# Retention attention and a maxout network: one plain feature block instead of two in the second tile, the weight sums moved forward, and the sums put in another order

## The chip, the cores and the metric

The kernel runs on one core of a Trainium2 chip. The metric is the device time of one execution in microseconds; a kernel's time is the median of its runs. In the profile PE is TensorE (PEld its weight loads), DVE is VectorE, ACT is ScalarE, POOL is GpSimd and SP is the queue that issues most of the transfers.

## The reference, cut to what matters

```python
# attention: batch 8, heads 8, seq 576, head_dim 64
scores = scale * np.matmul(q, k.transpose(0, 1, 3, 2))
Dmat = np.where(rel >= 0, gamma[:, None, None] ** rel[None, :, :], 0.0)
x = np.matmul(scores * Dmat, v)                 # then (B,H,S,D) -> (B*S, H*D)
# network: 4608 tokens, d_model 512, d_ff 768
h = np.maximum(np.maximum(x @ w1, x @ w2), x @ w3)
out = h @ w_out
```

The weights come in as 64-bit floats and are turned into 32-bit floats on the chip. All arithmetic that concerns us is in 32-bit floats.

## The kernel before, in words

**Tiles and blocks.** The 4608 tokens are cut into nine tiles `t` of 512. The 768 hidden features are cut into six blocks `fb` of 128. For each tile the function `ffn(t)` computes the hidden values `h[:, fb, :]` block after block, and then multiplies them by `w_out` (`downs`). Attention for the next tile (`scores`, `state`, `values`, `transposes`) is threaded in between: `ffn` is a generator that yields at set points, and the main loop (L755) issues the attention steps of `steps(t + 1)` at these points. Nothing is reordered later: each engine runs its instructions in the order in which the program issued them.

**Plain and fast blocks.** A block needs a product of a 2x4 grid (two halves of the tile's tokens by four chunks of d_model; the pieces are called `a11` to `a24`) with a 4x3 grid (four chunks by three weight matrices; `b11` to `b43`). Done plainly this is 24 small products. `up_plain` does it so: one triple (i = 0, 1, 2) of four 512-column products each. `up` does it with 20 products of 256 columns (`PRODUCTS`) at the price of sums before and after them. The sums of x (`X_SUMS`, 13 VectorE instructions for each tile, L335) and the sums of w (`W_SUMS`, 19 instructions, done in place in the weights, L530) come before. After the products, ScalarE copies partial results out of PSUM (L564), and VectorE joins them in 14 instructions (`JOINS`, L559), two of which write the block's hidden values: `lo` for the first 256 tokens (at product B6) and `hi` for the others (at product A7). The first tile (t = 0) is all plain, since its weights are still being converted. The second tile (t = 1) has two plain blocks, 2 and 3. From then on all blocks are fast.

**Accumulators.** A plain triple takes PSUM tiles from the pool `ps_x` (even fb) or `ps_y` (odd fb), each with two buffers. A fast block takes its chains A and B from `ps_x` and E, C and D from `ps_y`. A buffer comes free when its last reader is done: for a plain product with i = 0 a ScalarE copy (L604), for i = 1 and 2 a VectorE maximum (L603).

**Chores.** Sums that can wait are put into a queue `chores`, and `chore(n)` issues n of them. `urgent` is a second queue that goes first. Both mostly feed VectorE, and what is issued stands in VectorE's line before whatever comes after it.

**The down product.** `downs` computes `h @ w_out` by seven products over 2x2 grids, each over the three pairs `fp` of blocks. Product 1 (`dx`, L424) takes for each pair the `lo` half of the even block (e = 0) as its weights; product 2 (`dy`) takes the `lo` half of the odd block (e = 1). Products 3, 5, 6 and 7 take sums of the hidden values (`sums_of_hidden`, L400 to L402).

**Order of the blocks.** Two, three, zero, one, four, five in the second tile, and zero, one, four, five, two, three in all later tiles (L635).

Of the kernel before, what the change touches and what calls it, by code (L numbers as in the profile page):

```python
# [53 lines left out]
FILL = 224  # L54
PARTS = 20

X_SUMS = """s19 = a12 + a14, s15 = s19 - a22, s3 = a22 - a12, s10 = s3 - a13, s13 = a12 + a13, s20 = s10 + a23,
            s14 = a24 - s15, s11 = s20 + a24, s11 = a21 - s11, s7 = s11 - s13, s6 = s19 + s7,
            s16 = a11 - s11, s16 = s16 - a14"""
W_SUMS = """b33 = b13 + b33, n1 = b13 + b43, n2 = n1 - b41, n3 = b11 - n2, n4 = b33 - b32, b43 = b43 + n4,  # L60
            b23 = b43 - b23, b43 = b41 - b43, n5 = b22 + b23, b41 = b41 - n5, b21 = b21 - b41,
            b23 = b32 + b23, b22 = b22 - b21, b32 = b22 - b32, n6 = b31 + n2, n7 = b42 + n4,
            b42 = b42 - n5, b31 = b31 + b32, n8 = b12 - n4"""

PRODUCTS = """E a11 b12, E a14 b42, B s15 n5, A a22 b21, C s3 b23, B s19 b41, A s10 b32, C a13 b31, B s6 n2, A s13 b22,
              C a11 b11, B s14 n1, A s11 n4, D s7 b43, B a23 n6, A s20 b33, D s16 b13, B a21 n3, A a21 n8, A a24 n7"""
# [6 lines left out]
         "A7": [("A1", ("A1", "B6"), ALU.add), ("A1", ("A1", "A5"), ALU.max), ("hi", ("A1", "A7"), ALU.max)]}  # L73
X_SUMS, W_SUMS = ([x.split() for x in text.split(",")] for text in (X_SUMS, W_SUMS))
PRODUCTS = [x.split() for x in PRODUCTS.split(",")]
# [4 lines left out]
def kernel(  # L80
# [91 lines left out]
    late, chores, urgent, spread = {}, deque(), deque(), []  # L172

    def chore(n=1):
        for _ in range(n):
            if urgent or chores:
                (urgent or chores).popleft()()  # L177

    def soon(step):

        if spread:
            urgent.append(step)
        else:
            step()  # L184
# [135 lines left out]
    def output(chunks, o, t, i):  # L320
# [9 lines left out]
        if i == CPT - 1 and t > 0:  # L330
# [4 lines left out]
            def step(n, dst, _, a, sign, b):  # L335
                combine(*(xS[t][x] for x in (dst, a, b)), sign)
                if dst not in (later[0] for later in X_SUMS[n + 1:]):
                    made[t].add(dst)

            for n, line in enumerate(X_SUMS):  # L340
                soon(partial(step, n, *line))

    def combine(dst, a, b, sign):
        nc.vector.tensor_tensor(dst, a, b, op=ALU.add if sign == "+" else ALU.subtract)
# [31 lines left out]
    def sums_of_outs():  # L376

        pool = late["pool"]
        lo, hi = slice(0, DM // 2), slice(DM // 2, DM)
        b11, b12, b21, b22 = (w_out[:, :, e, r] for e in range(2) for r in (lo, hi))  # L380
        t1, t2, t4 = (pool.tile([P, NF // 2, DM // 2], FP32, name=f"To{n}")[:] for n in (1, 2, 4))

        def on_vector(fp):
            nc.vector.tensor_tensor(t1[:, fp], b12[:, fp], b11[:, fp], op=ALU.subtract)
            nc.vector.tensor_tensor(t2[:, fp], b22[:, fp], t1[:, fp], op=ALU.subtract)

        def on_gpsimd(fp):
            nc.gpsimd.tensor_tensor(b12[:, fp], b22[:, fp], b12[:, fp], op=ALU.subtract)
            nc.gpsimd.tensor_tensor(t4[:, fp], b21[:, fp], t2[:, fp], op=ALU.subtract)

        for fp in range(NF // 2):
            chores.extend([partial(on_vector, fp), partial(on_gpsimd, fp)])
        late["T"] = {1: b11, 2: b21, 3: b22, 4: t4, 5: t1, 6: t2, 7: b12}
        late["S"] = {n: pool.tile([P, NF // 2, NH], FP32, name=f"H{n}") for n in (1, 2, 3, 4)}
# [126 lines left out]
    def factor(name, fb):  # L521

        if name[0] == "n":
            return late["W"][int(name[1]) - 1][:, fb, :]
        d, i = int(name[1]) - 1, int(name[2]) - 1
        return w_up[i][:, fb, d * P:(d + 1) * P]

    summed_fp = set()

    def weight_sums(fp):  # L530

        def step(dst, a, sign, b):
            combine(*(factor(n, slice(2 * fp, 2 * fp + 2)) for n in (dst, a, b)), sign)

        for dst, _, a, sign, b in W_SUMS:
            chores.append(partial(step, dst, a, sign, b))
        chores.append(partial(summed_fp.add, fp))

    def late_room():
        pool = late["pool"]  # L540
        late["W"] = [pool.tile([P, NF, P], FP32, name=f"n{n}") for n in range(1, 9)]
        late["X"] = {n: pool.tile([P, NH], FP32, name=n)[:] for n in sorted({x[0] for x in X_SUMS})}

    converting = convert_all()

    def convert(n):
        for _ in range(n):
            next(converting, None)
# [35 lines left out]
    def downs_plain(t, h):  # L584

        ps = [(ps_x, ps_y)[m % 2].tile([P, DM], FP32, tag="xy"[m % 2], name="down") for m in range(NT // P)]
        for fb in range(NF):
            for m, b in enumerate(ps):
                nc.tensor.matmul(b[:], lhsT=h[:, fb, m * P:(m + 1) * P], rhs=w_sb["out", fb],
                                 start=(fb == 0), stop=(fb == NF - 1))  # L590
                if fb == NF - 1:
                    osb = opool.tile([P, DM], FP32, tag="osb", name="osb")
                    nc.scalar.copy(osb[:], b[:])
                    nc.sync.dma_start(out[t * NT + m * P:t * NT + (m + 1) * P, :], osb[:])
            yield

    def up_plain(t, h, fb, i):
        ps = (ps_x, ps_y)[fb % 2].tile([P, NT], FP32, tag="xy"[fb % 2], name="up")
        for dc in range(NDC):
            nc.tensor.matmul(ps[:], lhsT=w_sb[i, fb][:, dc * P:(dc + 1) * P], rhs=xT[t][:, dc, :],  # L600
                             start=(dc == 0), stop=(dc == NDC - 1))
        if i > 0:
            return lambda: nc.vector.tensor_tensor(h[:, fb, :], h[:, fb, :], ps[:], op=ALU.max)  # L603
        return lambda: nc.scalar.copy(h[:, fb, :], ps[:])  # L604

    def ffn(t):

        h = hpool.tile([P, NF, NT], FP32, tag="h", name="h")
        if t == 0:
            for fp, i in units:  # L610
                for fb in (2 * fp, 2 * fp + 1):
                    maximum = up_plain(t, h, fb, i)
                    convert(4)
                    maximum()
                yield
            convert(6)
            for fb, _ in enumerate(downs_plain(t, h)):
                convert(4 if fb < 2 else 4 * len(pieces))
                if fb == 2:
                    while_converting.close()  # L620
                    late["pool"] = ctx.enter_context(tc.tile_pool(name="late", bufs=1))
                    late_room()
                    sums_of_outs()
                elif fb > 2:
                    chore(2)
                if fb in (1, 3):
                    yield
            yield
            return
        if t == 1:  # L630
            spread.append(True)
            weight_sums(0)
            weight_sums(2)
        plain = (2, 3) if t == 1 else ()
        order = (2, 3, 0, 1, 4, 5) if t == 1 else (0, 1, 4, 5, 2, 3)  # L635
        total = sum(24 if fb in plain else len(PRODUCTS) for fb in order)
        count = parts = 0
        for n, fb in enumerate(order):
            if fb not in plain:
                while fb // 2 not in summed_fp:  # L640
                    chore()
            steps_of_one = up_plain_all(t, h, fb) if fb in plain else up(t, h, fb)
            for step, cost in enumerate(steps_of_one):
                if fb in plain:
                    chore(8)
                elif step % 2 or step % 5 == 4:
                    chore(len(urgent) > 0)
                elif step % 4 == 2 and chores:
                    chores.popleft()()
                count += cost or 1  # L650
                if count * (NF // 2 * 3) >= (parts + 1) * total:
                    parts += 1
                    yield
            if n % 2:
                sums_of_hidden(h, fb // 2)
                if fb in plain:
                    weight_sums(fb // 2)
        chore(len(urgent))
        for n, _ in enumerate(downs(t, h)):
            chore(4)  # L660
            if n in (1, 3):
                yield
        yield

    def up_plain_all(t, h, fb):
        for i in range(3):
            up_plain(t, h, fb, i)()
            yield 8
# [86 lines left out]
    for t in range(N // NT):  # L755
        work = ffn(t)
        for todo in steps(t + 1):
            for step in todo:
                step()
            next(work, None)  # L760
# [51 lines left out]
```

## Time and profile before

| | |
|---|---|
| median of 3 runs | 781.73 us (780.21 to 782.14) |
| span of the profiled run | 777.6 us |
| PE busy | 767.2 us, 99% |
| DVE busy | 569.7 us, 73% |
| ACT busy | 326.0 us, 42% |
| POOL busy | 101.9 us, 13% |
| granted TensorE clock | 1.00 |
| second tile, plain blocks | 124.50 to 147.28 us on PE |
| second tile, fast blocks | 147.28 to 189.90 us on PE |

The first tile ends at about 124 us of the span; each later one takes about 82 us. The busy time of PE is modelled for the ends of its instructions, so its gaps are read from the starts of instructions that follow each other.

### The profile page before, as it was taken

The page shows a single profiled execution, that of the slowest core. Times are in us where ns is not written, and L with a number is a line of the kernel's source. Part 1 is how long each engine was busy: PE and PEld are TensorE (multiplying, and loading weights), DVE is VectorE, ACT ScalarE, POOL GpSimd, SP SyncE. Part 2 cuts the span into 40 slices and gives each one's busy share as a digit, 9 for nine tenths or more (in the row PEclk, how much of TensorE's full clock was granted, in tenths as well). Part 3 has the DMA queues.
Part 4 walks back from the last instruction along what each step waited for, and adds up shares of the span by engine and source line. Part 5 has one row for each costly group of instructions (what it writes and reads, how often), then busy time and mean ns, then how long its engine had stood idle before and what let it go on. Part 6 is the DMA issues. An engine that isn't in the chain of part 4 may idle for free.

```text
span 777.6 us, 14439 instructions
## 1 busy us (share of the span) xinstructions
PE 767.2 (99%) x5000; PEld 624.4 (80%) x5000; DVE 569.7 (73%) x1248; ACT 326.0 (42%) x808; POOL 101.9 (13%) x124
## 2 busy tenths in 40 slices
PE   8899999999999999999999999999999999999998
PEld 7545444588888888888888888888888888888887
DVE  2998989889667857785769657876778567855672
ACT  3664641154155514452345234532544054524651
POOL 3110112101101201111111111110112001200000
PEclk9999999999999999999999999999999999999999
DMA  9995544333233332343233333333333323001001
GB/s 224 231 236 130 155 109 104 59 58 59 73 69 59 58 67 62 62 78 68 60 56 59 57 94 59 58 58 96 59 56 59 72 54 72 11 14 42 2 1 54
DMA packets 236939, 59.33 MB, mean 76 GB/s; under 512 B 217921, under 2 KB 235585, under 8 KB 236865
## 3 DMA queue, kind: packets, MB, share of 16 engines
q1 hardware_dynamic: 236432, 58.14, 34.9%
q8 instruction: 39, 0.64, 0.3%
q10 hardware_dynamic: 432, 0.27, 0.1%
q14 instruction: 36, 0.29, 0.1%
HBM read 48.89 MB, written 9.44 MB: 75 GB/s over the span
## 4 chain that ended last, share of the span: by engine, by line
PE 84%; DVE 6%; SPq 5%; DMA 3%; issue 1%; DVEq 0%; ACT 0%
PE a L579 17%; PE b L579 15%; PE dx L424 11%; PE c L579 8%; PE dz L424 5%; PE d L579 5%; PE e L579 5%; PE up L600 5%; SPq L195 4%; PE s L240 4%; PE o L296 3%; PE dy L424 3%; PE o L309 2%; PE kv L260 2%; DMA kraw<-in_k_dram 1%
## 5 line engine op out<-in xcount | busy, mean ns | idle before, releaser
L559 DVE TENSOR_TENSOR part<-part 128x256 f32<-128x256 f32 x460 | 210.0, 465 | 77.8 <-ACT part L564 70.0
L564 ACT COPY part<-a 128x256 f32<-128x256 f32 x276 | 102.7, 372 | 85.0 <-PE a L579 73.6
L564 ACT COPY part<-b 128x256 f32<-128x256 f32 x230 | 85.6, 372 | 125.9 <-PE b L579 116.0
L600 PE MATMUL up<-xT,w 128*128 128x512 f32 x192 | 84.5, 596 | 0.5 <-DVE xT L184 0.5
L579 PE MATMUL a<-s,w 128*128 128x256 f32 x276 | 82.3, 380 | 0.0
L579 PE MATMUL b<-s,n 128*128 128x256 f32 x276 | 82.1, 379 | 0.0
L211 POOL TENSOR_TENSOR vd<-vraw,gk 128x512 f32<-128x512 f32 x36 | 39.6, 1099 | 322.6 <-DMA vraw<-in_v_dram 283.0
L600 PEld LDWEIGHTS up<-xT,w 128*128 128x128 f32 x192 | 35.8, 190 | 43.4 <-issue 39.9
L579 PEld LDWEIGHTS a<-s,w 128*128 128x128 f32 x276 | 52.3, 190 | 7.3 <-issue 0.2
L579 PEld LDWEIGHTS b<-s,n 128*128 128x128 f32 x276 | 52.5, 190 | 7.1
L579 PE MATMUL c<-xT,w 128*128 128x256 f32 x184 | 56.0, 386 | 0.0
L579 PE MATMUL b<-xT,n 128*128 128x256 f32 x184 | 55.4, 382 | 0.0
L579 PE MATMUL d<-s,w 128*128 128x256 f32 x184 | 55.3, 382 | 0.1
L579 PE MATMUL a<-xT,n 128*128 128x256 f32 x184 | 47.2, 379 | 0.0
L579 PE MATMUL e<-xT,w 128*128 128x256 f32 x184 | 47.2, 379 | 0.0
L559 DVE TENSOR_TENSOR h<-part 128x256 f32<-128x256 f32 x92 | 41.2, 448 | 6.6
L424 PE MATMUL dx<-To,H 128*128 128x256 f32 x192 | 44.8, 383 | 0.0
L431 ACT COPY part<-dx 128x256 f32<-128x256 f32 x32 | 10.5, 375 | 80.0 <-PE dx L424 79.9
L177 DVE TENSOR_TENSOR xT<-o,gq 128x512 f32<-128x512 f32 x28 | 18.1, 686 | 33.1 <-PE o L309 33.1
L269 POOL TENSOR_TENSOR state<-state,gs 128x256 f32<-128x256 f32 x24 | 18.9, 785 | 172.9 <-DVE state L268 172.9
L424 PEld LDWEIGHTS dx<-To,H 128*128 128x128 f32 x192 | 35.9, 190 | 5.7 <-issue 1.0
L240 PEld LDWEIGHTS s<-qT,kT 64*128 64x128 f32 x576 | 33.7, 188 | 8.0 <-PE b L579 4.0
(104 smaller groups left out, 1301.2 us busy)
## 6 DMA issues: line engine op xcount, KB each, us to landing
bits<-in_moe_w_dram SPq DMA_DIRECT2D x36, 256.0 KB, 5.1
out_dram<-osb SPq DMA_DIRECT2D x35, 256.0 KB, 2.1
kraw<-in_k_dram SPq DMA_DIRECT2D x32, 256.0 KB, 3.0
vraw<-in_v_dram SPq DMA_DIRECT2D x32, 256.0 KB, 3.5
qraw<-in_q_dram SPq DMA_DIRECT2D x464, 16.0 KB, 1.8
kxraw<-in_k_dram SPq DMA_DIRECT2D x464, 16.0 KB, 1.8
bits<-in_moe_w_out_dram SPq DMA_DIRECT2D x6, 512.0 KB, 5.4
qraw<-in_q_dram SPq DMA_DIRECT2D x6, 256.0 KB, 4.7
```

Source lines behind the costliest of these rows:

```text
L177: (urgent or chores).popleft()()
L195: nc.sync.dma_start(t[32 * a:32 * a + 32, :, blk, :], src[b, a // 2::2, pos:pos + 32, 32 * (a % 2):32 * (a % 2) + 32].rearrange("p j i -> ...
L211: nc.gpsimd.tensor_tensor(t[:], raws.pop(("v", g))[:], gk[:].unsqueeze(2).to_broadcast([C, H, D]), op=ALU.mult)
L240: nc.tensor.matmul(s[j][:, p, :], lhsT=kT[r, p, :], rhs=qT[r, p, :], start=True, stop=True)
L260: nc.tensor.matmul(kvs[g][half(h % 2), h // 2, :], lhsT=kr[r:, h, :], rhs=vds[g][r:, h, :], start=True, stop=True)
L269: nc.gpsimd.tensor_tensor(t[:], t[:], gs[:], op=ALU.mult)
L296: nc.tensor.matmul(o[n % 2][half(c), m, n // 2, :], lhsT=vds[g][:, h, :], rhs=sts[g][:, h % 2, h // 2, :], start=m == 0 and n < 2, stop=be ...
L424: nc.tensor.matmul(out[m], lhsT=hS[n](fp)[:, m * P:(m + 1) * P], rhs=late["T"][n][:, fp, :], start=first and fp == 0 and (m == 0 or last a ...
L559: nc.vector.tensor_tensor(out, a, b, op=op)
L564: nc.scalar.copy(t[:], ps[step[0]][:])
L579: nc.tensor.matmul(ps[chain][:], lhsT=factor(w, fb), rhs=xS[t][x], start=n == 1, stop=ends, skip_group_check=True)
L600: nc.tensor.matmul(ps[:], lhsT=w_sb[i, fb][:, dc * P:(dc + 1) * P], rhs=xT[t][:, dc, :], start=(dc == 0), stop=(dc == NDC - 1))
```

## The change

It has four parts.

1. In the second tile only block 2 is plain; block 3 is now fast. The blocks stand in the order 2, 0, 1, 4, 5, 3, and in all later tiles in the order 0, 1, 4, 5, 3, 2.
2. The sums of w are made for any run of blocks: together for 0 and 1 and for 4 and 5, singly (128 columns instead of 256) for 3 and 2. Those for 0 and 1 are queued already in the last products of the first tile, in place of the sums of `w_out`, which move behind the sums of w for block 3. `chore(2)` becomes `chore(7)` there, and `chore(8)` becomes `chore(9)` after each plain product.
3. In a fast block two more steps (0 and 8) issue a chore.
4. `X_SUMS` and `W_SUMS` hold the same sums in another order, so that few of them take the result of the one just before.

It is for replacing a plain block by a fast one with less TensorE work, and for having the sums ready for it.

```diff
-X_SUMS = """s19 = a12 + a14, s15 = s19 - a22, s3 = a22 - a12, s10 = s3 - a13, s13 = a12 + a13, s20 = s10 + a23,
-            s14 = a24 - s15, s11 = s20 + a24, s11 = a21 - s11, s7 = s11 - s13, s6 = s19 + s7,
-            s16 = a11 - s11, s16 = s16 - a14"""
+X_SUMS = """s19 = a12 + a14, s3 = a22 - a12, s15 = s19 - a22, s10 = s3 - a13, s13 = a12 + a13, s20 = s10 + a23,
+            s14 = a24 - s15, s11 = s20 + a24, s11 = a21 - s11, s7 = s11 - s13, s16 = a11 - s11, s6 = s19 + s7,
+            s16 = s16 - a14"""
-W_SUMS = """b33 = b13 + b33, n1 = b13 + b43, n2 = n1 - b41, n3 = b11 - n2, n4 = b33 - b32, b43 = b43 + n4,
-            b23 = b43 - b23, b43 = b41 - b43, n5 = b22 + b23, b41 = b41 - n5, b21 = b21 - b41,
...
+W_SUMS = """b33 = b13 + b33, n1 = b13 + b43, n4 = b33 - b32, n2 = n1 - b41, b43 = b43 + n4, n3 = b11 - n2,
+            b23 = b43 - b23, n7 = b42 + n4, n5 = b22 + b23, b43 = b41 - b43, b41 = b41 - n5, b23 = b32 + b23,
...
-    def weight_sums(fp):
+    def weight_sums(*fbs):
         def step(dst, a, sign, b):
-            combine(*(factor(n, slice(2 * fp, 2 * fp + 2)) for n in (dst, a, b)), sign)
+            combine(*(factor(n, slice(fbs[0], fbs[-1] + 1)) for n in (dst, a, b)), sign)
...
-                    sums_of_outs()
+                    weight_sums(0, 1)
                 elif fb > 2:
-                    chore(2)
+                    chore(7)
...
         if t == 1:
             spread.append(True)
-            weight_sums(0)
-            weight_sums(2)
-        plain = (2, 3) if t == 1 else ()
-        order = (2, 3, 0, 1, 4, 5) if t == 1 else (0, 1, 4, 5, 2, 3)
+            weight_sums(4, 5)
+            weight_sums(3)
+            sums_of_outs()
+        plain = (2,) if t == 1 else ()
+        order = (2, 0, 1, 4, 5, 3) if t == 1 else (0, 1, 4, 5, 3, 2)
+        left = set(order)
...
-                while fb // 2 not in summed_fp:
+                while fb not in summed:
                     chore()
...
                 if fb in plain:
-                    chore(8)
+                    chore(9)
                 elif step % 2 or step % 5 == 4:
                     chore(len(urgent) > 0)
-                elif step % 4 == 2 and chores:
+                elif (step % 4 == 2 or step in (0, 8)) and chores:
                     chores.popleft()()
...
-            if n % 2:
+            left.remove(fb)
+            if fb ^ 1 not in left:
                 sums_of_hidden(h, fb // 2)
-                if fb in plain:
-                    weight_sums(fb // 2)
+            if fb in plain:
+                weight_sums(fb)
```

More of the change, by code (lines that the diff above doesn't have):

```diff
@@ L55 @@
 PARTS = 20
-X_SUMS = """s19 = a12 + a14, s15 = s19 - a22, s3 = a22 - a12, s10 = s3 - a13, s13 = a12 + a13, s20 = s10 + a23,
-            s14 = a24 - s15, s11 = s20 + a24, s11 = a21 - s11, s7 = s11 - s13, s6 = s19 + s7,
-            s16 = a11 - s11, s16 = s16 - a14"""
-W_SUMS = """b33 = b13 + b33, n1 = b13 + b43, n2 = n1 - b41, n3 = b11 - n2, n4 = b33 - b32, b43 = b43 + n4,
-            b23 = b43 - b23, b43 = b41 - b43, n5 = b22 + b23, b41 = b41 - n5, b21 = b21 - b41,
-            b23 = b32 + b23, b22 = b22 - b21, b32 = b22 - b32, n6 = b31 + n2, n7 = b42 + n4,
-            b42 = b42 - n5, b31 = b31 + b32, n8 = b12 - n4"""
+X_SUMS = """s19 = a12 + a14, s3 = a22 - a12, s15 = s19 - a22, s10 = s3 - a13, s13 = a12 + a13, s20 = s10 + a23,
[3 more added lines that the diff above has]
+            b23 = b43 - b23, n7 = b42 + n4, n5 = b22 + b23, b43 = b41 - b43, b41 = b41 - n5, b23 = b32 + b23,
+            b21 = b21 - b41, b42 = b42 - n5, b22 = b22 - b21, n6 = b31 + n2, b32 = b22 - b32, n8 = b12 - n4,
+            b31 = b31 + b32"""
 PRODUCTS = """E a11 b12, E a14 b42, B s15 n5, A a22 b21, C s3 b23, B s19 b41, A s10 b32, C a13 b31, B s6 n2, A s13 b22,
@@ L526, in factor @@
         return w_up[i][:, fb, d * P:(d + 1) * P]
-    summed_fp = set()
-    def weight_sums(fp):
+    summed = set()
+    def weight_sums(*fbs):
         def step(dst, a, sign, b):
-            combine(*(factor(n, slice(2 * fp, 2 * fp + 2)) for n in (dst, a, b)), sign)
+            combine(*(factor(n, slice(fbs[0], fbs[-1] + 1)) for n in (dst, a, b)), sign)
         for dst, _, a, sign, b in W_SUMS:
             chores.append(partial(step, dst, a, sign, b))
-        chores.append(partial(summed_fp.add, fp))
+        chores.append(partial(summed.update, fbs))
     def late_room():
```

## The prediction

> **What bounds the kernel now.** I read the page's busy times first, then the table of windows for PE, then PE's timeline wherever a window holds less than its length, and last VectorE's timeline at those places and at the ends of tiles. The page and the windows:
>
> ```profile
> PE 767.2 (99%) x5000; PEld 624.4 (80%) x5000; DVE 569.7 (73%) x1248; ACT 326.0 (42%) x808; POOL 101.9 (13%) x124
> ```
> ```profile
> 140.00:160.00 20.00, 18.31 (x138) 12.64 (x135) 15.49 (x34) 3.76 (x11) 2.87 (x3) 1.00 0.33 58
> 160.00:200.00 40.00, 39.94 (x285) 34.68 (x283) 37.11 (x87) 17.73 (x48) 6.12 (x7) 1.00 0.35 66
> 200.00:700.00 500.00, 500.00 (x3422) 436.72 (x3421) 358.18 (x806) 204.17 (x556) 65.31 (x76) 1.00 0.30 61
> ```
> After the window's length, the columns are PE, PEld, DVE, ACT and POOL busy. From 200 us on PE has no gap at all: there the kernel is a row of matmuls, and a saving elsewhere is worth nothing. The second tile (124.5 to about 210) has one gap, and in it VectorE is nearly full (37.11 of 40). The gap, on PE and on VectorE:
>
> ```profile
> 148.57 0.59 PE L579 MATMUL a<-xT,w 128*128 128x256 f32 x2
> 150.85 0.70 PE L579 MATMUL c<-s,w 128*128 128x256 f32 x2 [1.69 <-DVE h L603]
> 151.39 0.59 PE L579 MATMUL b<-s,w 128*128 128x256 f32 x2
> ```
> ```profile
> 150.12 0.68 DVE L603 TENSOR_TENSOR h<-h,up 128x512 f32<-128x512 f32 x1
> ```
> Chain C of the first fast block needs the `ps_y` buffer of block 3's last triple, and the maximum that frees it (ends 150.80) stands behind weight sums. Products follow each other by 0.43 us (151.39, 151.82), so the B after C would have begun at 148.57 + 2 x 0.432 = 149.43 without the wait; it began at 151.39. **The wait costs 1.96 us.** It also gives a rule: the waiting product begins in effect at 151.39 - 0.432 = 150.96, 0.16 us after the instruction it waited for ended.
>
> The end of a later tile, VectorE and PE:
>
> ```profile
> 271.71 1.34 DVE L559 TENSOR_TENSOR part<-part 128x256 f32<-128x256 f32 x3 [0.57 <-ACT part L564]
> 273.09 0.42 DVE L559 TENSOR_TENSOR h<-part 128x256 f32<-128x256 f32 x1
> ```
> ```profile
> 270.67 0.59 PE L579 MATMUL d<-s,w 128*128 128x256 f32 x2
> 271.10 0.59 PE L579 MATMUL b<-xT,n 128*128 128x256 f32 x2
> 271.54 1.03 PE L579 MATMUL a<-xT,n 128*128 128x256 f32 x4
> 272.40 2.75 PE L424 MATMUL dx<-w_out,h 128*128 128x256 f32 x12
> 274.99 1.24 PE L424 MATMUL dy<-w_out,h 128*128 128x256 f32 x5
> ```
> The last block's `lo` is ready at 273.51, 1.11 us after product 1 (`dx`) began, and nobody suffers: the last block is 3, an odd one, whose `lo` is first read in `dy`, from 274.99 on. This end is not a backlog. VectorE was idle for 0.57 us before the three joins of D2, waiting for ScalarE's copy of D2; copy, three joins that each take the result before, and `lo` are a chain that no order shortens.
>
> [...] L603 stood behind sums it has nothing to do with. [...] the trace has a weight sum of 1.26 us instead of 0.42 at 129.55, beside the decay product on POOL (129.30, 1.22 us long), so 0.84 us for one meeting.
>
> **The change, part by part.**
>
> *The block that becomes fast.* Four triples before (124.50 to 138.32, 32 records, 0.432 us each) give 24 x 0.432 = 10.37 us for a plain block. A fast one has 20 products of (274.99 - 272.40)/6 = 0.4317: 8.63 us. PE has nothing else to do there, so all is gained: **-1.73 us.**
>
> *The old wait goes.* With block 2 alone plain, `ps_y` is not used by a triple in this tile: **-1.96 us.**
>
> *A new wait comes in the same place.* Block 2's three triples take the `ps_x` buffers 1, 2, 1; B1 of the next block takes 2 and A1 takes 1. So A1 waits for the maximum of the last triple. In the order of the changed kernel's instructions, VectorE has before it: 7 weight sums (they fill the 4.5 us idle before the `xT` product at 117.63 and cost nothing), `xT`, 13 sums of x, a state, two transposes, 12 weight sums, two transposes, 9 weight sums, the first maximum, 9 weight sums, then this maximum. Durations of before: from `xT` (117.63) to the end of the first transposes 7.86 us (125.49). Of 13 sums of x, 6 took the result just before and 2 do now; such a start comes after 0.455 us rather than 0.335 (119.28 to 119.63 against 118.83 to 119.28), so 4 x 0.12 = 0.48 less: 125.01. Then 12 x 0.336 = 4.03 (none of the new W_SUMS takes the last one's result), 1.22 for two transposes, 3.02, maximum 0.60, 3.02: the last maximum begins at 136.90. The POOL decay product still falls in there (its transfer is issued at 121.57, and lands 3.5 us later, at 125): +0.84. It ends at 137.74 + 0.68 = 138.42, and A1 begins at 138.58. PE would be there at 124.50 + 10.37 + 3 x 0.432 (E1, E2, B1) = 136.17. **+2.41 us**[...].
>
> *The rest of the second tile.* VectorE gains 14 joins (about 5.7 us of its time: `lo` at 273.09 and five joins to 275.21 give 0.42 each) and two parts of `w_out` sums, and loses two maxima (1.2), and some 3.6 us of weight sums: 53 of 256 columns with 20 waits on the last result made before are now 31 of 256 and 31 of 128. No 128-column sum is in this trace; [...] I take 0.20. So about +1 us of work in 1.3 us less time, against idle VectorE time of some 4 us (3.88 before 157.78). Before, it ran up to 2.5 us behind without holding PE, since E's buffer is wanted 12 products, 5 us, later. I take 0; the far end is 2 us.
>
> *The order 3, 2 in later tiles.* Now the last block is 2, an even one, and its `lo` is the weight of the third product of `dx`, not of `dy`. The third product is due 0.863 us after `dx` begins; `lo` ends 1.11, 1.10, 1.38, 1.12, 1.12, 1.12 and 1.11 us after it in the seven tiles from the third to the ninth (read as above), plus 0.16. Waits: 0.41, 0.40, 0.68, 0.42, 0.42, 0.42, 0.41. The instruction order shows the wait on exactly this `lo`, ahead of the third `dx`. PE is in order and nothing else is idle: **+3.16 us.** [...] The second tile ends with block 3 and has none of it.
>
> *At nothing.* The new order of X_SUMS in later tiles and the extra chore steps: VectorE is 72% busy there (358.18 of 500) and PE waits for neither.
>
> Sum: -1.73 - 1.96 + 2.41 + 3.16 = +1.88; 781.73 + 1.88 = **783.6 us.**
>
> **The rivals.**
> 1. *The `lo` wait isn't there or is hidden*[...]. For it: PE never waited at a tile's end before. Against: the wait is on record in the order, and D2 to `lo` is 2.84 us where six products give 2.59. Then -1.73 - 1.96 + 2.41 = -1.3: 780.4 us[...].
> 2. *VectorE becomes the bound of the second tile*, and PE stops for a join or for E's buffer. For it: 37.11 of 40 before, with six `w_out` sums on VectorE and six on POOL now inside the fast blocks, each meeting costing 0.2 to 0.8 us. Against: 5 us of slack for each buffer. Another 2 to 3 us: 786 us.
> 3. *The new wait is short*, because the decay product falls beside a transpose: 0.84 less, 782.7 us.
>
> **How the numbers follow.** My forecast 0.60, rival 3 0.16, rival 2 0.16, rival 1 0.08. A change of 0.3% is 2.35 us, so the edges are 779.4 and 784.1. My forecast has spread of about 1 us[...], so a quarter of it (0.15) lies above 784.1, and nearly all of rival 2 (0.14); of rival 1 0.03 lies below 779.4. Faster 0.03, same 0.68, slower 0.29. The range takes in rival 3 and reaches down to just short of 781 and up to rival 2's near end: 781.2 to 785.8.
>
> **What would show it.** Right: in each tile from the third on, a gap of about 0.4 us on PE before the third `dx` record pair, laid to DVE `h` L560 (the line after the change); a gap of about 2 us at A1 in the second tile, laid to the maximum of L604, and none at C1; `dx` of the second tile beginning about 1.3 us earlier than 189.90. Wrong: no gap at `dx` (then rival 1), or gaps in the second tile behind joins (rival 2). Were the whole change faster than 779.4, the end-of-tile term would be wrong.

## The result, and the profile after

The changed kernel takes 790.8 us (median of 4 runs, 788.02 to 792.64), the kernel before, run beside it, 780.97 us (780.02 to 782.14). The ratio is 1.0122, with a 95% interval of 1.0087 to 1.0157: 9.8 us slower. The forecast was 783.6 us, and its range ended at 785.8. The sign was right and the size wrong by a factor of five.

The page of the changed kernel, part 1, and below it the table of windows (length, then PE, PEld, DVE, ACT and POOL busy, granted clock, DMA share, GB/s):

```profile
PE 773.9 (98%) x5016; PEld 631.4 (80%) x5016; DVE 572.9 (72%) x1279; ACT 330.8 (42%) x821; POOL 103.4 (13%) x124
```
```profile
140.00:160.00 20.00, 18.56 (x132) 16.15 (x134) 15.66 (x45) 7.82 (x21) 1.77 (x2) 0.91 0.32 58
160.00:200.00 40.00, 36.70 (x223) 31.49 (x219) 35.47 (x82) 17.87 (x48) 11.15 (x13) 0.96 0.30 54
200.00:700.00 500.00, 497.49 (x3429) 432.30 (x3428) 359.90 (x811) 203.69 (x554) 66.84 (x76) 1.00 0.30 61
```
Three things are new. PE now has gaps after 200 us, where it had none. It has 3.3 us of gaps from 160 to 200, where it had 0.06. And the granted clock, 1.00 in every one of these windows before, is 0.91 and 0.96 in the first two: PE was slower there, not only idle. PE's busy time over the span went up by 6.7 us although a plain block was replaced by a shorter fast one; a busy time that grows when work is taken out is a reason to read the clock.

**The first gap: A1 of the first fast block.** PE's timeline, and the maximum on VectorE's:

```profile
138.69 0.59 PE L580 MATMUL b<-s,n 128*128 128x256 f32 x2
141.44 0.70 PE L580 MATMUL a<-xT,w 128*128 128x256 f32 x2 [2.15 <-DVE h L604]
142.07 3.08 PE L241 MATMUL s<-qT,kT 64*128 64x128 f32 x32
145.08 1.22 PE L580 MATMUL c<-s,w 128*128 128x256 f32 x2
```
```profile
140.71 0.68 DVE L604 TENSOR_TENSOR h<-h,up 128x512 f32<-128x512 f32 x1
```
A1 could have begun at 138.69 + 0.43 = 139.12 and began at 141.44, counted by the start after it 141.64: 2.3 to 2.5 us, as forecast. But what comes next is slow as well. The 32 small products of the scores take 3.08 us where the kernel before took 2.06 (at 138.32), and the first product of chain C 1.22 us where one took 0.59 (a product is two records, x2). The clock in windows of 2 us:

```profile
142.00:144.00 2.00, 2.00 (x25) 1.93 (x26) 2.00 (x10) 0.37 (x1) 0.00 (x0) 0.72 0.24 36
144.00:146.00 2.00, 2.00 (x14) 1.69 (x12) 1.89 (x4) 0.00 (x0) 0.00 (x0) 0.50 0.23 35
146.00:148.00 2.00, 2.00 (x10) 1.70 (x10) 0.80 (x2) 1.12 (x3) 0.00 (x0) 0.93 0.77 173
```
PE is busy for the whole of all three. The clock that is missing is 2 x (0.28 + 0.50 + 0.07) = 1.7 us of full-speed time: 3.4 us at half clock. This gap cost its own length and 1.7 us more.

**The second gap: D1 of a later fast block.** PE, then VectorE and POOL:

```profile
178.74 0.59 PE L580 MATMUL a<-s,n 128*128 128x256 f32 x2
182.64 0.70 PE L580 MATMUL d<-s,w 128*128 128x256 f32 x2 [3.31 <-DVE part L560]
```
```profile
171.89 0.95 DVE L385 TENSOR_TENSOR To<-w_out 128x256 f32<-128x256 f32 x1
172.88 0.83 DVE L386 TENSOR_TENSOR To<-w_out,To 128x256 f32<-128x256 f32 x1
173.63 0.94 DVE L560 TENSOR_TENSOR part<-part 128x256 f32<-128x256 f32 x1
174.50 0.41 DVE L560 TENSOR_TENSOR part<-c,part 128x256 f32<-128x256 f32 x1
174.83 3.12 DVE L560 TENSOR_TENSOR part<-part 128x256 f32<-128x256 f32 x4
...
180.90 0.42 DVE L560 TENSOR_TENSOR h<-part 128x256 f32<-128x256 f32 x1
...
182.21 0.38 DVE L560 TENSOR_TENSOR part<-e,part 128x256 f32<-128x256 f32 x1
```
```profile
172.52 0.91 POOL L389 TENSOR_TENSOR w_out<-w_out 128x256 f32<-128x256 f32 x1
...
175.13 0.91 POOL L390 TENSOR_TENSOR To<-w_out,To 128x256 f32<-128x256 f32 x1
175.99 1.22 POOL L212 TENSOR_TENSOR vd<-vraw,gk 128x512 f32<-128x512 f32 x1
```
D1 takes the PSUM buffer that E held, and the join of E frees it. ScalarE's copy of B1, the other input of that join, was there at 175.43; the join began at 182.21, 6.8 us later, because VectorE was still at the joins of the block before. Two things had put it behind. Six sums of `w_out` stand among these joins, which in the kernel before were done by 128.06, ahead of any join (169.98 to 170.76, 171.89 to 173.63, 179.13 to 179.93: 3.3 us). And their four partners on POOL, with a decay product after them, run without a break from 172.52 to 177.2, so that joins of 0.42 us become 0.94, and four of them 3.12 us where four take 1.67 at the end of a later tile: 0.5 + 1.4 us more. Together 5.2 us, all of the slack of 5 us that the prediction gave E's buffer; and the same join of the block before, at 169.67, had come some 2.9 us after its copy already. In this trace 718 sums and joins of 256 columns (L345, L385, L386, L401, L402, L560) have no POOL instruction beside them, and none of these takes over 0.43 us; of the 120 that have one, 58 take longer, up to 1.32 us. D1 lost 3.6 us (178.74 + 0.43 = 179.17 against 182.75, counted back from the next start, 183.18), and again the clock drops:

```profile
182.00:184.00 2.00, 1.36 (x6) 1.23 (x7) 2.00 (x5) 0.37 (x1) 2.00 (x4) 0.96 0.23 35
184.00:186.00 2.00, 2.00 (x7) 1.56 (x6) 2.00 (x7) 0.74 (x2) 0.81 (x1) 0.50 0.22 33
186.00:188.00 2.00, 2.00 (x8) 1.66 (x7) 1.79 (x6) 0.72 (x2) 0.00 (x0) 0.69 0.85 194
```
Missing: 2 x (0.04 + 0.50 + 0.31) = 1.7 us.

**The ends of the later tiles.** From the first `dx` to the first `dy` there were 2.59 us before. Now there are 3.00, 3.01, 3.76, 3.00, 3.89, 3.00 and 3.00 us in the third to ninth tile: 4.53 us more in all. One of the two long ones, on PE, VectorE and POOL:

```profile
447.55 1.99 PE L425 MATMUL dx<-w_out,h 128*128 128x256 f32 x8 [0.91 <-DVE h L560]
```
```profile
444.93 2.11 DVE L560 TENSOR_TENSOR part<-part 128x256 f32<-128x256 f32 x3 [1.30 <-ACT part L565]
```
```profile
444.80 1.04 POOL L212 TENSOR_TENSOR vd<-vraw,gk 128x512 f32<-128x512 f32 x1 [10.14 <-DMA vraw<-in_v_dram]
```
A decay product on POOL falls on the three joins of D2 (2.11 us instead of 1.34), so `lo`, which waits for them, comes 0.8 us later and `dx` with it.

**The account.** The second tile, from its first plain product to its first `dx`, takes 198.27 - 127.53 = 70.74 us against 65.40: +5.34. The named parts give -1.73 - 1.96 + 2.4 + 1.7 + 3.6 + 1.7 = +5.7. From there to the end it is +4.9, of which 4.53 stand at the `dx`. The first tile is 3.0 us longer in this run: a transfer of keys landed late (a gap of 2.78 us before 24.09), and the clock is halved from 23.41 to 30.24. Half clock at that place, in attention steps that the change does not touch, is in nine of the twelve traces. It differs between the runs of one program: the kernel before has no half clock in its trace, and granted clocks from 0.993 to 1.00 in 52 other runs. No account is made of it. The three parts give the 13.3 us between the two profiled runs (790.9 and 777.6 us); the profiled run of the changed kernel was the longest of its four, so the sums below, read from this one trace, can't close exactly on the medians.

### The profile page after: what moved, and what is told of

Same layout as the page of the kernel before. It is cut to its first block, busy times and chain, and to the rows that moved or that the text cites. A ratio compares the mean times of both kernels' runs of the same rounds, so it can differ in the third digit from the quotient of the medians.

```text
span 790.9 us, 14519 instructions
## 1 busy us (share of the span) xinstructions
PE 773.9 (98%) x5016; PEld 631.4 (80%) x5016; DVE 572.9 (72%) x1279; ACT 330.8 (42%) x821; POOL 103.4 (13%) x124
## 4 chain that ended last, share of the span: by engine, by line
PE 90%; DVE 5%; DMA 3%; SPq 1%; issue 1%; ACT 0%; DVEq 0%
PE a L580 17%; PE b L580 15%; PE dx L425 10%; PE up L601 8%; PE c L580 8%; PE dz L425 5%; PE d L580 5%; PE e L580 5%; PE s L241 4%; PE o L297 4%; PE dy L425 3%; PE o L310 2%; PE kv L261 2%; PE down L590 2%; DVE part L560 2%; DMA qraw<-in_q_dram 1%
## 5 line engine op out<-in xcount | busy, mean ns | idle before, releaser
L560 DVE TENSOR_TENSOR part<-part 128x256 f32<-128x256 f32 x470 | 213.1, 462 | 82.7 <-ACT part L565 74.8
L565 ACT COPY part<-a 128x256 f32<-128x256 f32 x282 | 104.9, 372 | 87.6 <-PE a L580 76.9
L565 ACT COPY part<-b 128x256 f32<-128x256 f32 x235 | 87.4, 372 | 127.8 <-PE b L580 120.9
L580 PE MATMUL a<-s,w 128*128 128x256 f32 x282 | 84.1, 380 | 0.0
L580 PE MATMUL b<-s,n 128*128 128x256 f32 x282 | 83.9, 379 | 0.0
L601 PE MATMUL up<-xT,w 128*128 128x512 f32 x168 | 73.9, 595 | 0.5 <-DVE xT L185 0.5
L601 PEld LDWEIGHTS up<-xT,w 128*128 128x128 f32 x168 | 31.4, 190 | 38.2 <-issue 34.8
L580 PE MATMUL d<-s,w 128*128 128x256 f32 x188 | 57.0, 385 | 3.3 <-DVE part L560 3.3
L580 PE MATMUL a<-xT,n 128*128 128x256 f32 x188 | 48.9, 383 | 0.0
L560 DVE TENSOR_TENSOR h<-part 128x256 f32<-128x256 f32 x94 | 42.7, 455 | 7.4 <-ACT part L565 0.5
L580 PEld LDWEIGHTS d<-s,w 128*128 128x128 f32 x188 | 35.5, 191 | 9.7 <-DVE part L560 5.1
```

What stands on the lines that cost most here:

```text
L560: nc.vector.tensor_tensor(out, a, b, op=op)
L565: nc.scalar.copy(t[:], ps[step[0]][:])
L580: nc.tensor.matmul(ps[chain][:], lhsT=factor(w, fb), rhs=xS[t][x], start=n == 1, stop=ends, skip_group_check=True)
```

## The experiments

Two theories stood after this. *Mine*: the +9.8 us are three separate things, the waits at `dx` (about 4.5), the D1 wait made by the `w_out` sums meeting POOL in the fast blocks (3.6 + 1.7), and the A1 wait (2.4 + 1.7), with half clock behind the two long gaps. *The rival*: VectorE has too much to do in the second tile as a whole, so that a wait taken away in one place comes back in another, and the low clock is a chance of the run.

**The order of the later tiles put back** (changed kernel):

```diff
-        order = (2, 0, 1, 4, 5, 3) if t == 1 else (0, 1, 4, 5, 3, 2)
+        order = (2, 0, 1, 4, 5, 3) if t == 1 else (0, 1, 4, 5, 2, 3)
```


> The changed kernel with the order of blocks in the later tiles back at 0, 1, 4, 5, 2, 3. Theory (the time is lost in four places: the wait for the last block's lo in seven tiles, 4.5 us by the trace of after; the wait for a join at D1 in the second tile, 3.6 us; the wait at A1, 2.4 us; and a stretch of half clock after each of the two long gaps, 1.6 and 1.7 us): the seven waits at the third dx are gone, dx to dy takes 2.59 us in each tile, and the time falls by 4 to 5 us against after. Rival (VectorE is behind as a whole, and a wait taken away at dx comes back at dy or later): it falls by under 1.5 us.

Measured: 786.25 us (785.2 to 786.87; the kernel before beside it 780.78), ratio 1.0068, interval 1.0045 to 1.0091. That is 4.55 us less than the changed kernel, and no `dx` waits for an `h` any more. The two gaps of the second tile stay (2.17 and 3.32 us), each with 1.7 us of clock missing behind it.

**The order of the later tiles alone** (kernel before):

```diff
-        order = (2, 3, 0, 1, 4, 5) if t == 1 else (0, 1, 4, 5, 2, 3)
+        order = (2, 3, 0, 1, 4, 5) if t == 1 else (0, 1, 4, 5, 3, 2)
```


> The kernel before with one thing of the change: the order 0, 1, 4, 5, 3, 2 in the later tiles. Theory: seven waits of 0.41 us at the third dx, some of them up to 1.3 us where POOL delays the joins: 3.0 to 4.5 us slower than before, with the clock at 1.00. Rival (the wait arises only with the backlog that the rest of the change makes): no slower than 1 us.

Measured: 783.23 us (781.62 to 784.78), ratio 1.0031, interval 1.0021 to 1.0042: +2.45 us. The waits view of this run has one line for it (us in total, times, longest):

```profile
PEld dx L424 <- DVE h L559: 3.8, 7, 0.6
```
Seven waits, one in each later tile, none above 0.6 us: here no decay product falls on the joins of D2. The cost is near the 3.16 us of the prediction, though under the 3.0 us at which this run's expectation began. In the changed kernel the same line reads 5.5, 7, 1.4. So the order costs some 2.5 to 3 us by itself, and the rest of the 4.5 is the two meetings with POOL, which depend on where attention stands.

**The sums of `w_out` back in the first tile** (changed kernel). The last pairs are summed before the first tile's down product has read them, so this kernel's first tile comes out of weights that are partly sums already.

```diff
+                    sums_of_outs()
                     weight_sums(0, 1)
...
             weight_sums(3)
-            sums_of_outs()
```


> The changed kernel with the sums of w_out issued first, in the last products of the first tile, as before the change, and not inside the fast blocks. Theory: it is these six VectorE and six POOL sums[...] that put VectorE behind in block 4; without them there the 3.6 us wait at D1 and its 1.7 us of half clock are gone, and the wait at A1 grows by 0 to 1 us: 4 to 5.5 us less than after. Rival (the joins of one more fast block and the one-block sums are what fills VectorE): a wait of 2 us or more at a D1 or E1 stays, and the time falls by under 2 us.

Measured: 786.15 us (784.65 to 787.32), ratio 1.0068, interval 1.0046 to 1.0091: 4.65 us less than the changed kernel. With no sums of `w_out` among the joins, D1 goes so on PE's timeline:

```profile
178.20 0.59 PE L580 MATMUL a<-s,n 128*128 128x256 f32 x2
178.94 0.70 PE L580 MATMUL d<-s,w 128*128 128x256 f32 x2
```
It was due at 178.20 + 0.43 = 178.63: 0.3 us are lost instead of 3.6, and the clock is 1.00 from 178 to 182. The gap at A1 is as it was (2.44 us, half clock behind it). One wait went, and it did not come back elsewhere in the second tile. The sums on VectorE and their partners on POOL were moved together, so this run does not say which of the two weighs more.

**No sums between the second and the third triple** (changed kernel): the last maximum no longer stands behind nine sums.

```diff
-                    chore(9)
+                    chore((9, 0, 9)[step])
```


> The changed kernel with no weight sums issued between the last two maxima of the plain block (9, 0 and 9 chores after its triples instead of 9 each). Theory: VectorE comes to the last maximum 3.0 us earlier, so A1's wait of 2.4 us is gone, and with the gap its half clock (1.6 us); the nine sums are done later, where VectorE has idle time: 3 to 4 us less than after. Rival 1 (half clock comes by itself, not from a gap): only 2.4 us less, and a half-clock stretch stays near 142 us. Rival 2: the nine sums come back as a longer wait at D1, and nothing is gained.

Measured: 782.91 us (781.0 to 786.84), ratio 1.0029, interval 1.0018 to 1.0039: 7.9 us less than the changed kernel, twice what was expected. PE at A1 and at D1, and at the one gap that is new:

```profile
137.23 0.59 PE L580 MATMUL a<-xT,w 128*128 128x256 f32 x2
137.76 2.06 PE L241 MATMUL s<-qT,kT 64*128 64x128 f32 x32
...
174.40 0.70 PE L580 MATMUL d<-s,w 128*128 128x256 f32 x2 [0.35 <-DVE part L560]
...
193.08 1.99 PE L425 MATMUL dy<-w_out,h 128*128 128x256 f32 x8 [1.12 <-DVE h L560]
```
A1 follows at once, and the scores after it take 2.06 us. D1 waits 0.35 us, although the `w_out` sums are still in the second tile: nine sums fewer done early means that the `w_out` sums come nine places later in the queue. The first of them now begins at 176.26, after the join that D1 waits for. They take up about the same stretch as before (176.26 to 187.10, against 169.98 to 180.00 in the changed kernel), but the last two pairs fall in the tile's last block, behind which no other fast block of the tile wants a buffer, and there `dy` waits 1.1 us for a `lo`. With 2.4 + 1.7 at A1 and 3.0 + 1.7 at D1, less 1.1 at `dy`, 7.7 us are accounted for. So the D1 wait is not a matter of how much VectorE has to do in the tile, which is the same here. It is a matter of what stands in front of the join when it is wanted.

**A longer gap in the kernel before.** If half clock is the price of a long gap, then lengthening the gap of 1.69 us that the kernel before has, by three additions whose result nothing uses, must cost more than the length added:

```diff
+        if t == 1 and fb == 3 and i == 2:
+            idle = ppool.tile([P, NH], FP32, tag="part", name="idle")
+            for _ in range(3):
+                nc.vector.tensor_tensor(idle[:], xT[t][:, 0, 0:NH], xT[t][:, 1, 0:NH], op=ALU.add)
```


> The kernel before with three extra VectorE additions of 256 columns (results unused) ahead of the maximum that its one gap waits for, so that the gap grows from 1.7 to about 2.7 us. Theory (a gap of over about 2 us is followed by some 3.4 us at half clock): 1.0 us for the longer wait and 1.7 us for the half clock, 2.7 us slower than before, with half clock from about 152 us on. Rival (half clock comes by chance or from something else in the changed kernel): 1.0 us slower and the clock 1.00 there.

Measured: 783.37 us (781.57 to 786.96, 20 runs; before 780.92), ratio 1.003, interval 1.0016 to 1.0043: +2.45 us for 1.1 us of gap. PE, and the windows behind it:

```profile
157.16 0.78 PE L579 MATMUL c<-s,w 128*128 128x256 f32 x2 [2.78 <-DVE h L607]
```
```profile
158.00:160.00 2.00, 2.00 (x6) 1.55 (x6) 0.77 (x3) 1.04 (x3) 0.73 (x1) 0.50 0.22 34
160.00:162.00 2.00, 2.00 (x18) 1.34 (x18) 0.76 (x2) 0.42 (x2) 0.00 (x0) 0.74 0.22 33
```
With 0.18 us from the window ahead of these, 0.18 + 1.0 + 0.52 = 1.7 us of clock are missing again. So lengthening one gap brings the half clock, without anything else of the change. It is not there in every run: one stretch alone (1.7 of 783 us) takes the granted clock to 0.998, and one of the 20 runs has 0.999. The last section shows what it depended on in these traces.

**The new order of the sums alone** (kernel before with the `X_SUMS` and `W_SUMS` of the change):

> The kernel before with the new order of X_SUMS and W_SUMS alone. Theory: in the later tiles it is worth nothing, since PE doesn't wait for them; in the second tile the maximum that C1 waits for comes earlier by the starts that no longer take the last result (4 of X, 7 for each set of weight sums before it, 0.12 us each), 1 to 2 us, so most of the one gap of 1.96 us goes: 1 to 2 us faster than before. Rival: nothing that can be measured.

Measured: 780.32 us (778.66 to 784.69; before 780.92), ratio 0.9992, interval 0.9981 to 1.0004. PE's idle time ahead of C1 (at 151.29 in this trace) shrinks from 1.69 to 0.87 us. The 0.8 us agree with the 0.6 us by which the median fell, which by itself can't be told from nothing; the same gap is 1.48 us in the trace of the later order alone, where the sums are unchanged, so some 0.2 us of it varies by itself. The new order shortens the gap, by about half of what was expected; that the kernel is faster by it is not shown.

**Putting it together.** The changed kernel with the later order put back and no sums between the triples, that is the first and the fourth of these edits at once:

> The changed kernel with both cures: the order 0, 1, 4, 5, 2, 3 in the later tiles and no weight sums between the last two maxima. Theory (the two losses add): what the cure of the order gave against after (4.5 us) on top of what the cure of the maximum gave (7.9 us), so about 778 to 779.5 us, 1.5 to 2.5 us faster than before, with no gap at dx. Rival (VectorE only passes its backlog on): over 780.8, no faster than before.

Measured: 779.45 us (778.24 to 783.52, 14 runs; before 780.92), ratio 0.9989, interval 0.9975 to 1.0003: the two losses add, as expected. In its second tile the weight loads wait 0.8 us at each of two joins and 1.5 us at `dy`. The same with 12 instead of 9 sums after the last maximum:

> The kernel with the later order 2, 3 and no sums ahead of the last maximum, with 12 instead of 9 sums taken after that maximum. Three sums fewer are then left for the fast blocks, so the w_out sums come earlier: the wait of 1.5 us ahead of the second product of the second tile's end should shrink by about 1 us, and the waits of 0.8 us at the joins of block 0 stay or grow by the 0.6 us that three sums of 128 columns take. Expected 778.5 to 779.5 us. If VectorE's backlog only moves, 779.5 to 781 us; if E's join becomes late by over 2 us, half clock follows and it is 782 us or more.

Measured: 779.27 us (778.2 to 783.38, 14 runs; before 780.49), ratio 0.999, interval 0.9976 to 1.0004. The wait ahead of `dy` shrank (1.52 to 0.59 us) and one ahead of an E appeared (1.36 us): the backlog moved. At this size, of about 1 us, the rival theory holds. Both versions beat the changed kernel by 11 us; against the kernel before, the medians are 1.5 and 1.2 us lower and both intervals reach just past 1, so that they are faster than it is likely but not shown.

Two attempts to win the wait at `dy` as well failed. They put the sums of `w_out` back in the first tile, each pair behind the product that reads it, in the kernel with the later order put back. The first takes 2, 0 and 12 sums after the three triples (the diff shows these two parts of the edit; the places in the queue and the order of the later tiles are left out):

```diff
-                    weight_sums(0, 1)
+                    weight_sums(0, 1)
+                    sums_of_outs()
...
-                    chore(9)
+                    chore((2, 0, 12)[step])
```


> Both cures, and the sums of w_out back in the last products of the first tile (each pair only after the product that reads it), 2, 0 and 12 chores after the plain triples. Theory: it takes the last waits of the second tile away as well (E1 and D1 waits of 0.4 us each and a dy wait of 1.1 us in the kernel with the maximum first), so 776.5 to 778.5 us, 2.5 to 4 us faster than before. Rival: the w_out sums and their meetings with POOL make A1 wait again, 1 us or more, and it is no faster than the kernel with the two cures alone.

Measured: 783.85 us (782.41 to 785.85; before 780.92), ratio 1.0039, interval 1.0025 to 1.0054. PE:

```profile
184.82 1.19 PE L581 MATMUL a<-s,w 128*128 128x256 f32 x2 [3.36 <-DVE w L345]
```
Too few sums had been taken in block 2, and the last fast block waited for its own sums of w, with half clock behind. The second attempt takes 9, 0 and 12:

> The version that sums w_out in the first tile's last products waited 3.4 us in the last fast block of the second tile for that block's own weight sums, because only 14 of the queue's steps were taken in block 2. Here 9 are taken after the first triple of block 2 and 12 after its last maximum, so the weight sums of block 3 are done before block 3 begins. If that was the whole miss, the wait and the half clock behind it (3.4 + 1.7 us) go and the time is 778 to 779.5 us, about 2 us below the kernel before. If the meetings with GpSimd in the first tile's last products are what costs, the wait comes back ahead of the third triple or in the first fast block and the time is 781 to 784 us.

Measured: 782.02 us (779.38 to 783.94; before 780.49), ratio 1.0011, interval 0.9999 to 1.0024. That wait is gone, but another took its place, much as the second theory of its expectation had it, though the meetings with POOL stand in the second tile: in the first triples of block 2 the decay product and four `w_out` sums on POOL (127.84 to 134.44) stretch the sums of w from 0.42 to 0.95 and 1.26 us, and the last two maxima came late:

```profile
139.91 0.70 PE L581 MATMUL b<-s,n 128*128 128x256 f32 x2 [1.78 <-DVE h L605]
140.71 1.22 PE L581 MATMUL a<-xT,w 128*128 128x256 f32 x2
```
The second line, 1.22 us for one product, is at half clock already.

## Why the prediction was wrong

- *The block that becomes fast, -1.73, and the old wait, -1.96*: no separate run was made for them. The wait at C1 is gone from the trace, and the sum of the second tile closes to 0.4 us with both terms in it. The extra chore steps (part 3 of the change) had no run of their own either.
- *A new wait at A1, +2.41*: right (2.3 to 2.5), with the maximum and the cause as forecast; the one meeting with POOL cost 0.6 us (a sum of 1.01 us at 128.03) where 0.84 was taken. What stands behind it was missed: 1.7 us at half clock. The prediction knew of no cost after a gap, since the only gap it had to read, 1.69 us, has none behind it.
- ***The rest of the second tile, taken at 0 with a far end of 2 us***: this is the step that failed. It measured 3.6 us of waiting at D1 and 1.7 us of half clock behind. The prediction had the pieces, the six `w_out` sums on VectorE, their partners on POOL, 0.84 us for a meeting, and the slack of 5 us. But it weighed them as an amount of work against an amount of idle time in the whole stage, and did not line them up: all six sums and four partners fall within 10 us, in two blocks, where VectorE had hardly an idle moment. (The amount was also a little low: 5.7 and two sums of 0.42 gained against 1.2 and 3.6 lost come to 1.7 us, not 1.) The run without sums of `w_out` there shows the cause. The run without sums between the last two maxima, where the same six sums come behind the join that D1 waits for, shows that their place counts and not their amount. How the loss divides between the sums and their meetings with POOL is read from one trace only.
- *The order 3, 2 in later tiles, +3.16*: the mechanism was right, and five of the seven waits are 0.41 or 0.42 us, as forecast. The term is 4.5 us in the changed kernel, since two of them are 1.2 and 1.3 us where POOL meets the joins. By itself, on the kernel before, the order costs 2.45 us.
- *At nothing* (order of the sums): right for the later tiles; the 0.20 us from start to start of a sum of 128 columns, the author's estimate, is what the trace has (141.64, 141.84).
- *The rivals*: the second one, VectorE becoming the bound of the second tile, is the nearest. It was given 786 us and 0.16; with the half clock of both gaps (3.4) and the two meetings at `dx` (1.4) added it comes to 790.8. That this is the median to the digit is luck: the rival had 2 to 3 us for a wait that took 3.6. The first (no wait at `dx`) and the third (a short wait at A1) fell.

The change cost 9.8 us where the sum had 1.88. Of these 7.9 us, 5.3 are the D1 wait and its half clock, 1.7 the half clock behind A1, and 1.4 the two long waits at `dx`; together 0.5 more than the difference of the medians.

## What to carry to other kernels

Backlog is local: where an engine takes its instructions in order, as VectorE did here (the join of E began 6.8 us after its copy, behind the joins of the block before), and has slack measured in single buffers, line up the instructions of two or three blocks one by one, and with them what POOL does at the same time (beside it joins of 0.42 us took 0.94); totals over the stage hide it. A gap in TensorE's row of products cost its length here and, where 1.83 us or more of idle PE fell into one window of 3.413 us (see below), 1.7 us more, so an edit that lengthens a gap a little can cost a good deal: 1.1 us of gap cost 2.45 us. And before a last block is exchanged, ask which of its results is read first, and how soon.

## What the runs showed of the hardware that was not expected

In the traces of five kernels, gaps of PE of 2.15 us and more in the second tile were each followed by half clock (2.15 and 3.31, 2.17 and 3.32, 2.44, 2.78, 3.36 us): 3.4 us of it in all, 1.7 us lost, and twice as much after the last. Gaps of 1.69 us and less in that tile were not; behind one of 1.78 us, with a second short wait at the next product, it was there too.

The traces also show what it went with. Where one trace has several half-clock stretches, they begin whole multiples of 3.413 us apart (23.41, 142.88 and 183.84 us in the changed kernel; 183.84 - 142.88 = 40.96 = 12 x 3.413), and those that end before the program does last one, two or three times 3.413 us (142.88 to 146.29 and 23.41 to 30.24 us in the changed kernel, 10.24 us from 24.52 on in the trace of the longer gap). So in these traces half clock came and went on a grid of 3.413 us that the gaps did not move. Cut along this grid, the changed kernel reads:

```profile
139.47:142.88 3.41, 1.44 (x16) 1.11 (x18) 3.41 (x13) 0.60 (x2) 0.00 (x0) 1.00 0.23 34
142.88:146.29 3.41, 3.41 (x27) 3.01 (x24) 3.30 (x9) 0.00 (x0) 0.00 (x0) 0.50 0.23 34
177.02:180.43 3.41, 2.32 (x11) 1.71 (x9) 3.24 (x9) 1.62 (x5) 0.20 (x1) 1.00 0.22 33
180.43:183.84 3.41, 1.20 (x6) 1.07 (x7) 3.31 (x7) 0.37 (x1) 2.10 (x3) 1.00 0.23 34
183.84:187.25 3.41, 3.41 (x10) 2.70 (x9) 3.27 (x10) 1.12 (x3) 0.97 (x2) 0.50 0.39 77
```
The windows ahead of the two slow ones have PE idle for 3.41 - 1.44 = 1.97 and 3.41 - 1.20 = 2.21 us. The window at 177.02, which holds the first 1.09 us of the D1 gap, is followed by full clock. This can be counted over the whole span of the ten traces that have a half-clock stretch, and with it a known grid. Windows that reach past the program's start or end are left out, and PE's busy time is the modelled one. All 18 full-clock windows with 1.83 us or more of idle PE were followed by a slow one, and none of the other 2242, which have 1.39 us or less. Both edges stand in the trace of the later order alone, in the first tile: 1.39 us idle from 18.45 on, full clock after it; 1.83 us from 21.86 on, half clock after it. Between these two values no window was seen. A slow window was followed by another where PE was idle for 0.51 us or more of it, and by full clock where it was 0.40 us or less.

So what counts in these traces is not the length of a gap but how much of it falls into one window, and the same gap can cost 1.7 us more or nothing. The kernel with 9, 0 and 12 sums and `w_out` in the first tile shows it: its profiled run (782.88 us, the gap of 1.78 us in it) has two slow windows, and another run of it, with a granted clock of 1.00, takes 779.38 us. The difference of 3.5 us is two times 1.7 and leaves at most 0.1 us for a shorter gap.
